# Chunk inverse by Newton steps instead of doubling, one mask and the beta copies dropped, and new planning numbers, in a delta-rule attention and MLP kernel

## Chip, cores, metric

One core of one Trainium2 chip. The metric is device time in microseconds (us), median of several runs, lower is better. "Before" is the kernel that was changed, "after" the changed one. Engines have the names of the profile: PE multiplies matrices (PEld loads its weights), DVE, ACT and POOL work on tiles, and SP issues transfers. An eviction is the copy of a product out of PSUM, the memory that PE writes, by DVE or ACT.

## The reference, cut

```python
batch, n_heads, seq, head_dim = (4, 8, 768, 48)          # 32 heads
k_n = k / (norm(k) + 1e-6)
for t in range(S):                                        # delta rule, one state 48x48 per head
    y[t]  = q[t] @ state
    v_old = k_n[t] @ state
    state = state + beta[t] * outer(k_n[t], v[t] - v_old)
x = y as (3072, 384)
out = gelu_tanh(x @ w_in) @ w_out                         # 384 -> 2048 -> 384
```

## The kernel before

The sequence is cut into 12 chunks of 64 steps. In a chunk, the triangular system that couples its steps, T = (I + N)^-1 with N strictly triangular and 64x64, is solved for each of the 32 heads. The heads go in two groups of 16, so there are 24 chunk-groups. One batch is 16 products of 64x64, one for each head of the group. The inverse of different chunks is independent; the state (R, U, S) goes from chunk to chunk. After every two chunks 512 rows of attention output are ready for the MLP.

The program is not ordered by hand. Each piece of work is given to a planner with a cost for each engine that could do it; the planner places all pieces in time, and the order on each engine is then fixed. The costs matter for nothing else, but a wrong cost gives a bad order.

```python
LAT = {"pe": 0.25, "dve": 0.12, "act": 0.14, "pool": 0.16, "sp": 0.0}
...
late = max(0.0, t - free_at[e])
key = (late > 0.0, t if late > 0.0 else 0.0, o.prio, i)      # ready first, then earliest, then rank
...
def mm_pe(n_ins, cols):
    return {"pe": 0.02 + n_ins * max(0.030, (cols / 2.4 + 32) * 0.5e-3)}
...
# norm of k: the root costs the plan 0.6
op({"pool": 0.6}, {"pool": f_tt(sr[j][:, :], ss[j][:, :], half[:, :], ALU.pow)}, ...)
...
# two masked and scaled versions of K K^T: N (upper) and M (lower)
NU = mU * bcol          # POOL
ML = mL * brow          # POOL; brow is beta broadcast to 64 partitions by DMA, 2 x 256 KB a chunk
M0 = psum * ML          # DVE
N0 = psum * NU          # DVE
DT = psum * mU          # DVE
L1 = I - N0             # POOL
for j in range(0, 6):                # doubling (cut to its data flow)
    [N', L*] = M.T @ [N, L]          # one batch; 128 columns wide for j = 1, 2, 3
    M'       = N.T @ M               # one batch (j <= 4)
    N' evicted by ACT or DVE; L' = L* + L on DVE; M' evicted by ACT or DVE
```

Eleven batches a group, three of them 128 columns wide; DVE does three masks, five additions and a share of the nine plain evictions.

## Time and profile before

| | before |
|---|---|
| median of 4 runs | 403.9 us (402.66 to 407.32) |
| first matmul on K/Q | 52.0 us |
| state update of chunk 1 | 113.2 us |
| state update of chunk 10 | 348.3 us |
| 9 chunks between them | 235.1 us, 26.1 each |
| rest | 55.8 us |

The state updates (DVE, output S) are good milestones, since every chunk has one. I call the time until that of chunk 1 start and ramp, the 9 chunks after it steady state, and the rest the tail.

The page of before, head and slices. A digit is the busy share in a fortieth of the span (10 us); PEclk is the granted TensorE clock in tenths.

```profile
PE 293.8 (73%) x7110; PEld 195.6 (48%) x7110; DVE 256.3 (63%) x389; ACT 146.7 (36%) x247; POOL 163.5 (40%) x112
...
PE   0100062646668969869978979989889999889997
...
DVE  2101267679896965946966857988778797784102
...
POOL 3449358396864741741823533425034110110000
PEclk9999997568588888998979999999999999999999
```

Almost nothing happens on PE for an eighth of the span (1.7 us of work in 52), then it is half busy until slice 12, and from there it is nearly full. DVE is the next busiest in the middle.

The same by stages, from windows of the trace; the columns are window, length, then busy us with instruction counts of PE, PEld, DVE, ACT, POOL, then granted clock, DMA share, GB/s.

```profile
0.00:52.00 52.00, 1.67 (x10) 1.37 (x10) 7.88 (x18) 1.28 (x1) 25.86 (x26) 1.00 0.96 169
52.00:113.20 61.20, 35.73 (x1200) 32.18 (x1200) 48.55 (x69) 21.67 (x38) 45.99 (x29) 0.72 0.76 136
113.20:348.30 235.10, 205.56 (x5196) 132.46 (x5196) 177.56 (x271) 99.12 (x168) 89.28 (x56) 0.94 0.43 81
348.30:404.10 55.80, 50.84 (x708) 29.63 (x708) 22.33 (x34) 24.59 (x42) 2.31 (x2) 1.00 0.12 37
```

In steady state PE is idle for 235.1 - 205.6 = 29.5 us of 235, and DVE is 76% busy. What PE waits for in the whole span (releaser; us, times, longest):

```profile
PE ps L285 <- DMA KQT<-KQ: 41.2, 2, 32.0
PE ps L285 <- DVE NL L269: 22.6, 29, 3.8
```

and in the steady stage alone:

```profile
PE ps L285 <- DVE NL L269: 13.0, 18, 2.5
```

The first is the wait for the transposed K and Q. The second is the addition of L on DVE, one of the steps of the doubling; PE waits there for an eviction. The SP queue around the first transpose (start, us to issue, what):

```profile
39.90 2.11 SPq L293 DMA_DIRECT2D brow<-in_beta_dram  x2
42.06 3.56 SPq L293 DMA_DIRECT2D kf<-in_k_dram  x2
45.66 1.32 SPq L293 DMA_DIRECT2D vf<-in_v_dram  x1
47.02 3.12 SPq L292 DMA_TRANSPOSE KQT<-KQ  x1
```

The transpose of chunk 0 is issued behind the loads of three chunks, with three pairs of beta copies. The groups that the change touches most (busy us, mean ns | PE idle before, releaser):

```profile
L285 PE MATMUL ps<-M,NL 64*64 64x64 bf16 x1920 | 54.9, 202 | 10.2 <-issue 2.9 <-DVE NL L274 2.8 <-ACT M L278 2.3
L285 PE MATMUL ps<-NL,M 64*64 64x128 bf16 x1152 | 48.5, 232 | 17.8 <-DVE NL L269 10.8 <-DVE S L274 4.4 <-DVE M L274 1.0
...
L269 POOL TENSOR_TENSOR ML<-mL,brow 128x1024 f32<-128x1024 f32 x12 | 28.5, 2376 | 18.4 <-DVE M L269 12.5 <-DMA brow<-in_beta_dram 5.8
```

### The profile page before, as it was taken

What the parts mean: (1) busy time and instruction counts of PE and PEld (TensorE: products, weight loads), DVE (VectorE), ACT (ScalarE), POOL (GpSimd) and SP (SyncE); (2) the same over time, 40 slices, a digit from 0 to 9 for tenths busy, and PEclk for the clock granted to TensorE, in tenths of its full rate; (3) what the DMA queues carried; (4) which work ended last, traced back from release to release, by engine and by line L of the source; (5) the groups of instructions that cost most, each with busy time, mean ns of one, the idle gap of its engine ahead of it and who ended that gap; (6) DMA issues with size and microseconds to landing.
All of it is one profiled execution on the core that took longest, in us unless ns stands there. A gap on an engine that the chain in (4) does not pass through costs nothing.

```text
span 404.1 us, 15305 instructions
## 1 busy us (share of the span) xinstructions
PE 293.8 (73%) x7110; PEld 195.6 (48%) x7110; DVE 256.3 (63%) x389; ACT 146.7 (36%) x247; POOL 163.5 (40%) x112
## 2 busy tenths in 40 slices
PE   0100062646668969869978979989889999889997
PEld 0100062645565635645645644656556566565554
DVE  2101267679896965946966857988778797784102
ACT  1000033233355632413734515643067430664260
POOL 3449358396864741741823533425034110110000
PEclk9999997568588888998979999999999999999999
DMA  7998979888279640752722944227122031000302
GB/s 147 181 176 170 172 150 154 162 154 147 52 132 126 124 90 15 159 125 62 143 45 41 185 99 84 33 42 114 60 44 55 3 62 61 4 3 12 108 2 78
DMA packets 141039, 38.14 MB, mean 94 GB/s; under 512 B 135472, under 2 KB 140592, under 8 KB 140976
## 3 DMA queue, kind: packets, MB, share of 16 engines
q1 hardware_dynamic: 138464, 34.02, 44.8%
q0 software_dynamic: 2512, 3.15, 4.8%
q8 instruction: 56, 0.92, 1.0%
q14 instruction: 7, 0.06, 0.0%
HBM read 26.94 MB, written 4.72 MB: 78 GB/s over the span
## 4 chain that ended last, share of the span: by engine, by line
PE 40%; DVE 23%; POOL 20%; DMA 6%; SPq 4%; issue 4%; ACT 1%; DVEq 0%; POOLq 0%
PE ps L285 40%; POOL sr L269 8%; DVE NL L269 6%; POOL ML L269 5%; SPq L293 4%; DMA KQT<-KQ 3%; DVE NL L274 3%; POOL NU L269 3%; DVE M L269 2%; DMA kf<-in_k_dram 2%; POOL sq L269 2%; DVE ss L473 2%; DVE S L269 2%; POOL NL L269 1%; DVE ss L469 1%
## 5 line engine op out<-in xcount | busy, mean ns | idle before, releaser
L285 PE MATMUL ps<-NL,M 64*64 64x128 bf16 (+1 forms) x2304 | 81.5, 219 | 32.0 <-DVE NL L269 22.6
L285 PEld LDWEIGHTS ps<-NL,M 64*64 64x64 bf16 x2304 | 64.9, 118 | 53.3 <-DVE NL L269 31.2
L278 ACT ACTIVATE M<-ps 128x512 bf16<-128x512 f32 x90 | 52.8, 596 | 76.5 <-PE ps L285 76.1
L278 ACT ACTIVATE gT<-ps 128x512 bf16<-128x512 f32 x96 | 57.3, 597 | 62.5 <-PE ps L285 60.2
L285 PE MATMUL ps<-xT,W 128*128 128x512 bf16 x288 | 76.6, 401 | 2.4 <-DVE S L269 1.2
L285 PE MATMUL ps<-W,gT 128*128 128x384 bf16 x384 | 69.8, 331 | 1.7 <-DVE TT L269 0.8
L269 DVE TENSOR_TENSOR NL<-ps,NL 128x512 bf16<-128x512 f32 x96 | 64.4, 684 | 2.9 <-PE ps L285 1.3
L269 POOL TENSOR_TENSOR NL<-idI,NL 128x512 bf16<-128x512 f32 x24 | 27.8, 1160 | 85.9 <-DVE NL L269 85.9
L285 PE MATMUL ps<-M,NL 64*64 64x64 bf16 x1920 | 54.9, 202 | 10.2 <-issue 2.9
L278 ACT ACTIVATE NL<-ps 128x512 bf16<-128x512 f32 x44 | 26.2, 597 | 85.7 <-PE ps L285 85.4
L285 PEld LDWEIGHTS ps<-M,NL 64*64 64x64 bf16 x1920 | 44.6, 117 | 22.6 <-issue 7.3
L285 PEld LDWEIGHTS ps<-W,gT 128*128 128x128 bf16 x384 | 35.2, 99 | 25.4 <-issue 1.0
L285 PE MATMUL ps<-KQT 48*64 48x128 bf16 x384 | 11.7, 239 | 41.4 <-DMA KQT<-KQ 41.2
L269 POOL TENSOR_TENSOR KQ<-kf,rn 128x768 bf16<-128x768 f32 x12 | 17.7, 1474 | 57.0 <-PE ps L285 55.2
L274 DVE CAST NL<-ps 128x512 bf16<-128x512 f32 x52 | 35.2, 687 | 6.9 <-PE ps L285 5.8
L285 PEld LDWEIGHTS ps<-xT,W 128*128 128x128 bf16 x288 | 24.8, 101 | 30.4 <-issue 4.6
L269 POOL TENSOR_TENSOR sr<-ss,half 128x16 f32<-128x16 f32 x12 | 34.9, 2906 | 10.3 <-DVE ss L469 10.3
L269 POOL TENSOR_TENSOR ML<-mL,brow 128x1024 f32<-128x1024 f32 x12 | 28.5, 2376 | 18.4 <-DVE M L269 12.5
L274 DVE COPY osb<-ps 128x384 f32<-128x384 f32 x21 | 11.6, 554 | 32.2 <-PE ps L285 32.1
L285 PEld LDWEIGHTS ps<-KQT 48*64 48x64 bf16 x384 | 7.7, 117 | 45.4 <-DMA KQT<-KQ 41.6
L469 DVE TENSOR_REDUCE ss<-sq 128x16 f32<-128x768 f32 x12 | 11.4, 948 | 28.9 <-POOL sq L269 28.9
L269 DVE TENSOR_TENSOR M<-ps,ML 128x512 bf16<-128x512 f32 x24 | 16.3, 682 | 15.9 <-PE ps L285 15.9
(46 smaller groups left out, 267.9 us busy)
## 6 DMA issues: line engine op xcount, KB each, us to landing
brow<-in_beta_dram SPq DMA_DIRECT2D x24, 256.0 KB, 6.6
kf<-in_k_dram SPq DMA_DIRECT2D x24, 192.0 KB, 4.7
qf<-in_q_dram SPq DMA_DIRECT2D x24, 192.0 KB, 4.3
vf<-in_v_dram SPq DMA_DIRECT2D x24, 192.0 KB, 4.1
out_dram<-osb SPq DMA_DIRECT2D x24, 192.0 KB, 1.9
W<-in_moe_w_in_dram POOLq DMA_DIRECT2D x3, 512.0 KB, 7.9
W<-in_moe_w_out_dram POOLq DMA_DIRECT2D x2, 768.0 KB, 11.5
BL<-in_beta_dram SPq DMA_DIRECT2D x2, 96.0 KB, 3.3
```

The lines of the kernel that those rows point to most:

```text
L269: return lambda e: e.tensor_tensor(out() if callable(out) else out, a() if callable(a) else a, b() if callable(b) else b, op)
L274: return lambda e: e.tensor_copy(out, a() if callable(a) else a)
L278: return lambda e: e.activation(out, a() if callable(a) else a, func)
L285: ins = t.matmul(out, lhsT, rhs, start=st, stop=sp_, skip_group_check=skip)
L293: return lambda e: e.dma_start(out, a)
L469: op({"dve": 0.95}, {"dve": lambda e: e.tensor_reduce(ss[j][:, :], sq[:, :, :], AX.X, ALU.add)}, reads=["sq"], writes=[f"ss{j}"], prio=pr)
L473: op({"dve": 0.1}, {"dve": lambda e: e.tensor_scalar(ss[j][:, :], sr[j][:, :], 1e-6, None, op0=ALU.add)}, reads=[f"sr{j}"], writes=[f"ss{j ...
```

## The change

The inverse becomes five Newton steps, Z' = (2I - Z X) Z with X = (I + N).T, transposed once on PE. Every step has two batches of products, both 64 columns wide, an eviction on DVE (F = 2I - ZX) and one on ACT. Neither M nor the second mask nor the beta copies are needed any more. Beside that: squares and q copies may go to ACT; the root of the first three chunks is a Sqrt on ACT; the output x is evicted by ACT only; intermediate tiles get three buffers. The planner gets new costs, new latencies, a cost for changing between 64x64 and 128x128 matmuls (SWITCH), and a rule that treats work that is late by less than NEAR as ready. The core of the diff, cut:

```diff
-LAT = {"pe": 0.25, "dve": 0.12, "act": 0.14, "pool": 0.16, "sp": 0.0}
+LAT = {"pe": 0.22, "dve": 0.06, "act": 0.06, "pool": 0.08, "sp": 0.0}
+SWITCH = 0.095
+NEAR = {"pe": 0.3, "dve": 0.05, "act": 0.05, "pool": 0.0, "sp": 0.0}
...
-                    key = (late > 0.0, t if late > 0.0 else 0.0, o.prio, i)
+                    far = late > NEAR[e]
+                    key = (far, t if far else 0.0, pr, i)
...
-            op({"pool": 0.6}, {"pool": f_tt(sr[j][:, :], ss[j][:, :], half[:, :], ALU.pow)},
+            if c < NSQ:
+                op({"act": 0.24}, {"act": f_act(sr[j][:, :], ss[j][:, :], ACT.Sqrt)}, ...
+            else:
+                op({"pool": 2.95}, {"pool": f_tt(sr[j][:, :], ss[j][:, :], half[:, :], ALU.pow)}, ...
...
-            op(d_pool2(NP * C), {"pool": f_tt(ML[j][:, :, :], mL..., brow[i][:, :, :], ALU.mult)}, ...
...
-        def mm_pe(n_ins, cols):
-            return {"pe": 0.02 + n_ins * max(0.030, (cols / 2.4 + 32) * 0.5e-3)}
+        def mm_pe(n_ins, cols, tiles=2):
+            t = max(31.0, cols / 2.4 + 3.0) / tiles
+            return {"pe": 1e-3 * n_ins * max(8.3, t)}
...
-            for j in range(0, 6):              # doubling: see above
+            # W = I + N and Z0 = I - N on POOL or DVE; X = W.T by a PE transpose, evicted on ACT
+            for j in range(5):
+                op(mm_pe(16, 64), {"pe": prod(h1, Zo, X)}, ...)
+                op(d_ps(512), {"dve": f_tt(F[:, :, :], bc(twoI), v1(h1), ALU.subtract)}, ...)
+                op(mm_pe(16, 64), {"pe": prod(h2, F, Zo)}, ...)
+                op(d_act(512), {"act": f_act(dst, v1(h2))}, ...)      # dst: Z', at last TT
```

## The prediction

> **What bounds the kernel.** Three stages (busy time by windows of the trace):
> - 0 to 52 us: PE does 1.7 us of work. The first real matmul waits 32 us for the first K/Q transpose (waits). The DMA engines are 0.96 busy with 192- and 256-byte packets; in SP's order the transpose stands behind three chunks of loads and their broadcast-beta copies.
> - 52 to 120 us: PE is busy 40 us of 68, at a granted clock of 0.73; DVE 55, POOL 51. POOL pays per chunk 2.9 (pow), 2.4 (second mask), 1.9, 1.5, 1.5, 0.8 and 2 x 1.16. The first MLP matmul starts at 123.5.
> - 120 to 404 us: PE-bound, 252 us busy of 284; about 26 us a chunk (steps of the S update).
>
> **What changes** (24 chunk-groups; durations from the groups of instructions).
> - PE: before, 11 batches of 16 products a group, three of them 128 columns wide; after, one transpose batch and 10 products, all 64 wide. A 128-wide batch shows 0.63 us, a 64-wide one 0.44: 72 x 0.15 to 0.2 = 11 to 14 us less. MLP (146 us) and state stay.
> - DVE: a group loses one 0.68 mask multiply and its share of evictions (82 x 0.69); x goes to ACT (11.5); some W/Z work comes: 256 to about 190-205 us.
> - ACT: 5.6 evictions a group become 6 (0.6 each); x, some squares and q copies come: 147 to 170-180.
> - POOL: loses the second mask (28.5) and three pows (8.7), shares sq and q copies, makes W and Z0 (2 x 1.16, or on DVE): 163 to 125-140.
> - DMA: 24 x 256 KB of 38 MB go.
> - Longer: the inverse becomes 10 dependent steps of about 0.44 + 0.65 + waits = 1.25 us, plus a transpose prologue: about 16 us a group instead of about 10. Three chunk buffers should hide this, except in the first chunk.
> - Sqrt on ACT costs one or two table loads: about 1283 ns each by the Trainium skill, "ScalarE: Activation LUTs", What ACT_TABLE_LOAD costs; the trace shows 1283. Negligible.
>
> **Critical path.**
> - Start: without 1.5 MB of beta copies for three chunks (9 us at 165 GB/s), and with a shorter norm chain, the first transpose lands at about 38-44 instead of 52: 8 to 14 us.
> - Ramp: POOL no longer limits; first MLP at about 95 instead of 123 in all (another 12 to 18 us net of the longer inverse). The Trainium skill, "TensorE: Matmul & The Clock Gate", Part 1, says that idle time halves the clock; the 0.73 agrees, and a denser ramp should raise it.
> - Steady: PE's 11 to 14 us count nearly in full; planning costs that fit the measured durations (pow planned at 0.6, took 2.9) should save 5 to 10 us of the 32 us of PE idle. Faster DVE and POOL give nothing here by themselves.
> Sum: 10 + 15 + 12 + 8 = 45 to 50 us. Predicted 357 us, range 335 to 379. Chances: faster 0.93, same 0.05, slower 0.02.
>
> **What would show it.** PE busy 275-283 us, above 77% of the span; first K/Q matmul before 45 us; first GELU before 102; DVE near 200; POOL below 140; near 24 us a chunk; no wait on beta loads.
>
> **What would make it wrong.**
> - SP may still place the first transpose behind three chunks: then the start gives under 5 us.
> - The longer chain on in-order ACT, behind GELUs, leaves PE waiting in mid-kernel: 370-385.
> - More switches between 64x64 and 128x128 matmuls (PE idle for "issue") could eat the PE gain.
> - A better plan could bring PE idle after the ramp near nothing: 335.

## The result and the profile after

| | before | after |
|---|---|---|
| median of 4 runs | 403.9 us | 343.4 us (342.62 to 346.65) |
| first matmul on K/Q | 52.0 | 41.3 |
| state update of chunk 1 | 113.2 | 92.8 |
| 9 chunks after it | 235.1 | 198.1 (22.0 each) |
| tail | 55.8 | 50.0 |

All outputs are right. The ratio is 0.851 (95% interval 0.843 to 0.858). Ratios here are the mean time of one kernel's fast runs over that of the other's of the same rounds, so not quite the ratio of the medians that I quote.

The page of after (a slice is 8.5 us):

```profile
PE 266.8 (78%) x7110; PEld 173.4 (51%) x7110; DVE 181.0 (53%) x287; ACT 169.5 (50%) x286; POOL 120.4 (35%) x90
...
PE   0001125875769999898999699999999999999896
...
DVE  2102255786774757676676554666757756642001
...
POOL 5007266443679616057432660160252105000000
PEclk9999999999678999999999699999999999999999
```

By stages, columns as above:

```profile
0.00:41.30 41.30, 1.69 (x10) 1.40 (x14) 6.87 (x21) 8.05 (x11) 13.71 (x19) 1.00 1.11 180
41.30:92.80 51.50, 32.57 (x1363) 29.61 (x1364) 34.72 (x57) 22.57 (x39) 26.99 (x17) 0.93 0.58 95
92.80:290.90 198.10, 187.08 (x5114) 116.83 (x5114) 126.24 (x192) 117.00 (x200) 79.71 (x55) 0.97 0.48 88
290.90:340.90 50.00, 45.49 (x639) 25.58 (x633) 13.21 (x20) 21.84 (x37) 0.00 (x0) 0.99 0.13 41
```

In steady state PE is busy for 187.1 us instead of 205.6, and idle for 11.0 instead of 29.5: busy time and idle time each gave 18.5 us. DVE fell from 76% to 64%.

The clock column needs a caution in the first two stages. In the kept traces the clock's record begins only with its first change, at 59.7 us in before and 67.2 in after, and the view counts time without a record as full clock. The batches of after say otherwise; one of 16 products of 64x64 before and one after that moment:

```profile
66.62 0.62 PE L296 MATMUL ps<-Z,F 64*64 64x64 bf16 x16
69.67 0.42 PE L296 MATMUL ps<-Z,F 64*64 64x64 bf16 x16
```

Batches in a stretch that is recorded at half clock also take 0.61 to 0.64 us (86 to 91 us). If the time before the first record is counted as half clock, my estimate from these records for the ramp is 0.66 in before and 0.68 in after, not 0.72 and 0.93.

The waits of PE, whole span, and then the steady stage alone (DVE F is the step that answers to the addition of L):

```profile
PE ps L296 <- DMA KQT<-KQ: 17.5, 3, 12.2
...
PE ps L296 <- DVE F L280: 1.8, 5, 0.9
```

```profile
PE ps L296 <- DVE F L280: 0.7, 3, 0.3
```

The queue before the first transpose, which still stands behind three chunks of loads, only without the beta copies:

```profile
32.03 2.12 SPq L304 DMA_DIRECT2D qf<-in_q_dram  x2
34.20 1.98 SPq L304 DMA_DIRECT2D vf<-in_v_dram  x2
36.22 3.45 SPq L303 DMA_TRANSPOSE KQT<-KQ  x1
```

And the products; there is no 128-wide group and no second mask any more:

```profile
L296 PE MATMUL ps<-Z,F 64*64 64x64 bf16 x1920 | 54.1, 201 | 7.2 <-issue 5.0 <-DVE F L280 1.8
L296 PE MATMUL ps<-X,Z 64*64 64x64 bf16 x1920 | 52.8, 201 | 8.9 <-ACT Z L289 4.8 <-POOL Z L280 2.4 <-issue 1.3
```

So about 20 us came before chunk 1's state, 37 in steady state and 6 in the tail. The prediction had 25 and 20. The total lies in its range, but steady state gave nearly twice what it said. That is what the experiments are about.

### The profile page after: what moved, and what is told of

Its sections match the earlier page's. It is cut to its first block, busy times and chain, and to the rows that moved or that the text cites. A ratio compares the mean times of both kernels' runs of the same rounds, so it can differ in the third digit from the quotient of the medians.

```text
span 340.9 us, 15121 instructions
## 1 busy us (share of the span) xinstructions
PE 266.8 (78%) x7110; PEld 173.4 (51%) x7110; DVE 181.0 (53%) x287; ACT 169.5 (50%) x286; POOL 120.4 (35%) x90
## 4 chain that ended last, share of the span: by engine, by line
PE 66%; SPq 12%; DMA 8%; ACT 5%; issue 3%; DVE 3%; POOL 1%
PE ps L296 64%; SPq L304 9%; DMA kf<-in_k_dram 7%; SPq L303 2%; ACT Z L289 2%; PE ps L571 2%; ACT x L289 1%; ACT sq L289 1%; DVE F L280 1%; DMA xT<-x 1%; POOL W L280 1%; DVE N L280 1%; DVE R L280 1%; POOL sq L280 0%; POOL Z L280 0%
## 5 line engine op out<-in xcount | busy, mean ns | idle before, releaser
L280 DVE TENSOR_TENSOR F<-twoI,ps 128x512 bf16<-128x512 bf16 x120 | 80.1, 683 | 55.1 <-PE ps L296 54.5
L289 ACT ACTIVATE Z<-ps 128x512 bf16<-128x512 f32 x96 | 55.3, 597 | 39.1 <-PE ps L296 38.7
L296 PE MATMUL ps<-X,Z 64*64 64x64 bf16 x1920 | 52.8, 201 | 8.9 <-ACT Z L289 4.8
L296 PE MATMUL ps<-Z,F 64*64 64x64 bf16 x1920 | 54.1, 201 | 7.2 <-issue 5.0
L280 POOL TENSOR_TENSOR W<-identB,N 128x512 bf16<-128x512 bf16 x21 | 24.2, 1151 | 95.3 <-DVE N L280 95.3
L296 PEld LDWEIGHTS ps<-Z,F 64*64 64x64 bf16 x1920 | 42.6, 115 | 28.7 <-DVE F L280 16.4
L296 PEld LDWEIGHTS ps<-X,Z 64*64 64x64 bf16 x1920 | 42.5, 116 | 25.0 <-ACT Z L289 13.9
L289 ACT ACTIVATE x<-ps 64x768 bf16<-64x768 f32 x24 | 19.3, 804 | 15.7 <-PE ps L296 15.3
L296 PE MATMUL ps<-KQT 48*64 48x128 bf16 x384 | 12.5, 246 | 18.5 <-DMA KQT<-KQ 17.5
L280 POOL TENSOR_TENSOR NU<-mU,bcol 128x1024 f32<-128x1024 f32 x12 | 23.7, 1976 | 1.0 <-DVE bcol L285 1.0
L289 ACT ACTIVATE TT<-ps 128x512 bf16<-128x512 f32 x24 | 14.1, 595 | 18.7 <-PE ps L296 18.6
L280 DVE TENSOR_TENSOR N<-ps,NU 128x512 bf16<-128x512 f32 x24 | 16.3, 686 | 11.8 <-PE ps L296 11.7
```

The lines of the kernel that those rows point to most:

```text
L280: return lambda e: e.tensor_tensor(out() if callable(out) else out, a() if callable(a) else a, b() if callable(b) else b, op)
L289: return lambda e: e.activation(out, a() if callable(a) else a, func)
L296: ins = t.matmul(out, lhsT, rhs, start=st, stop=sp_, skip_group_check=skip)
```

## Experiments

Each was timed in 3 rounds (the last one in 5) beside before on the same chip; before had medians of 403.0 to 404.9 us there, so medians can be compared between the jobs to about half a per cent. My theory after the result was that the gain is about half less work and half a better order. The rivals were that either of them is all of it.

### Control: how far does an accidental order move the time?

```diff
-LAT = {"pe": 0.22,
+LAT = {"pe": 0.23,
```

> A control: one planning latency of the new kernel moved by 0.01 us, no work changed. It shows how far an accidental other order of the same work moves the time. Expected within 1.5%: 338 to 348. If it moves by more than 6 us, differences of that size between other kernels can't be read as causes.

Measured: 347.3 us (343.34 to 348.11). The same work in a slightly different order is 4 us slower in the median. Below, 4 us mean nothing. It is one nudge only: every run below that adds work has another order too, and how far that moves the time is bounded only roughly.

### Work and order apart

The new kernel with all old planning numbers (only one MLP cost, 0.65 for 0.67, stays new):

```diff
-LAT, SWITCH, NEAR, d_ps, d_any, d_act, d_pool2, mm_pe, pow 2.95, reciprocal 0.25   # new
+LAT 0.25/0.12/0.14/0.16, SWITCH 0, NEAR 0, costs of before, pow 0.6, reciprocal 0.2
```

> The new inverse and the new data paths, ordered with all the old planning numbers (old latencies, old costs, no switch cost, no nearness rule). Theory: the 61 us come about half from less work (PE columns, evictions, second mask, beta copies) and half from the order that truer numbers give; then 365 to 382 us, with PE idle after the first 120 us back near 25 us. Rival A, the work alone: 340 to 352. Rival B, the order alone: 392 to 408.

Measured: 362.3 us (ratio 0.896), a little under the range of the theory.

The old kernel with the new planning numbers, rules and matmul kinds; its work is untouched:

```diff
-LAT = {"pe": 0.25, ...}; key = (late > 0.0, ...); pow 0.6; mm_pe old
+LAT = {"pe": 0.22, ...}; SWITCH, NEAR; pow 2.95; mm_pe new
```

> The old kernel with doubling, both masks and the beta copies, ordered with the new planning numbers and rules. Theory: 365 to 382 us, first K/Q matmul still near 50 us, PE idle between 120 us and the last chunk down from 27 us to under 15. Rival A, the work alone: 398 to 408. Rival B, the order alone: 340 to 352.

Measured: 372.9 us (ratio 0.921).

| ratio to before | old numbers | new numbers |
|---|---|---|
| doubling | 1 | 0.921 |
| Newton | 0.896 | 0.851 |

Both rivals fall. The work is worth 10.4% with the old plan and 7.7% with the new (0.851/0.921); the plan is worth 7.9% with the doubling and 5.1% with Newton (0.851/0.896). They overlap: together they save less than the sum. The steady stages of the two runs, first Newton with the old plan, then doubling with the new:

```profile
96.30:303.80 207.50, 188.06 (x5148) 117.58 (x5142) 122.53 (x187) 115.47 (x194) 76.81 (x55) 0.97 0.44 80
```

```profile
100.10:316.80 216.70, 200.49 (x5318) 132.13 (x5312) 174.22 (x269) 111.83 (x192) 109.10 (x68) 0.95 0.54 97
```

The work takes PE busy from 205.6 to 188.1 us; the order takes PE idle from 29.5 to 16.2 us without any change of the work. With the order alone PE's wait for the additions of L on DVE falls from 13.0 to 0.8 us in steady state, although DVE still does them and is busy for 80% of the stage; in the run of doubling with new numbers:

```profile
PE ps L293 <- DVE NL L277: 0.8, 2, 0.7
```

So the long wait for DVE in before came for the most part from the order, and does not show that DVE had too much to do.

### Which part of the plan: costs or rules?

The new kernel with the old costs of instructions, the new latencies and rules:

> The new kernel ordered with the old instruction costs, but the new latencies, switch cost and nearness rule. The old costs hold a batch of 16 products for 0.52 us of PE where the trace shows one every 0.25 us, and the pow for 0.6. Theory: the costs are most of what the plan is worth: 355 to 364, near the 362 of the run with all old numbers. Rival: latencies and rules are: under 348.

Measured: 370.2 us (ratio 0.917), 27 us slower than after and above the range of the theory.

The new kernel with the new costs, and LAT, SWITCH and NEAR as before:

> The new kernel with the new instruction costs but the old latencies, no switch cost and no nearness rule: the fourth corner beside the runs of 343, 362 (all old) and 370 (only costs old). If the costs alone make the order good: 340 to 350. If costs and rules need each other: 355 or more.

Measured: 353.6 us (ratio 0.877), between the two expectations.

The costs matter more, above all with the new rules: 370.2 to 343.4 with the new rules, 362.3 to 353.6 with the old. The rules are worth 10 us with true costs and cost 8 us with wrong ones, so they need the costs. What was wrong with the old costs can be read from the code and the trace. A batch of 16 products of 64 columns cost the old plan 0.02 + 16 x 0.030 = 0.50 us of PE, the new plan 16 x 15.5 ns = 0.25 us. In the trace of after, batches that follow each other start at this distance:

```profile
71.86 0.44 PE L296 MATMUL ps<-X,Z 64*64 64x64 bf16 x16
72.11 0.44 PE L296 MATMUL ps<-Z,F 64*64 64x64 bf16 x16
```

It is 0.25 us; the 0.44 us include the end of the last product, which the next batch covers. The old plan thus charged PE twice the time that these batches take at full clock (at half clock, before 67 us, they follow each other at 0.43 us). That it therefore saw PE as full and had no reason to bring another group's batch forward is my reading of the planner, and no run shows it. In the steady stage of the run with old costs PE is busy 196 and idle 23 us of 219:

```profile
94.70:314.00 219.30, 196.32 (x5152) 120.96 (x5152) 118.53 (x180) 113.39 (x193) 81.46 (x58) 0.96 0.41 76
```

I did not separate PE's costs from those of the other engines.

### What of the work: narrower products?

Three products of each group are 128 columns wide again; the second half is unread:

```diff
-    {"pe": prod(h2, F, Zo)},  alloc=[(h2, 1)]
+    wide = j in (1, 2, 3)     # rhs = both Z buffers, 128 columns; ACT evicts the half that counts
+    {"pe": f_mms(pw) if wide else prod(h2, F, Zo)},  alloc=[(h2, 2 if wide else 1)]
```

> The new kernel with three of the ten products of each group made 128 columns wide again (the other half of the result unread; the output stays right). Theory: PE is the limit in steady state, so the 72 wide batches cost 10 to 15 us: 353 to 359. Rival: the narrower products were hidden in PE idle time and give nothing: under 347. A wide product also takes two PSUM banks; if banks are what limits, over 362.

Measured: 348.8 us. PE busy rose by 8.8 us (275.6 instead of 266.8), the time by 5.4 us over after and by 1.5 over the control. Between the two expectations, and near the limit of what the control lets one read. The prediction counted 11 to 14 us "nearly in full". The products themselves did rise by about that: the group Z,F takes 66.3 us instead of 54.1. The rest of PE took less, at a higher mean granted clock (0.990 instead of 0.969), so the 8.8 us understate the work.

### What of the work: the load of DVE?

The change took 75 us of work from DVE. Here four extra multiplies a group go back to it, each bound between two F steps:

```diff
+                if j < 4:
+                    op(d_ps(512), {"dve": f_tt(scr, NU[j2][:, ps_, :], mU..., ALU.mult)},
+                       reads=[nm["F"], f"NU{j2}"] + MASKU, writes=["scr"], prio=pj + 0.15)
```

> The new kernel with four extra DVE multiplies a group (128x512, about 0.6 to 0.7 us each, into a tile that nobody reads), placed between the F steps: gives DVE back the roughly 60 us that the change took from it. The prediction said that a faster DVE gives nothing in steady state by itself: then under 349. Rival, suspected since the wide products cost only some 5 us: DVE, in order, was where the products of before waited, and its relief is a main part of the gain: 355 or more, with PE idle for DVE F up from 2 us to over 10.

Measured: 372.9 us (ratio 0.925), 29.5 us slower than after. The multiplies took 79 us in all, 0.82 each, more than I expected. Chunk 1's state came at 106.1 instead of 92.8 us, steady state took 207.2 instead of 198.1, the tail 56.7 instead of 50.0. So 13.3 us were lost before chunk 1's state, 9.1 in steady state and 6.7 in the tail. PE's wait for DVE F rose from 1.8 to 8.5 us over the span, less than the 10 of the expectation. The steady stage:

```profile
106.10:313.30 207.20, 193.62 (x5207) 121.92 (x5205) 170.61 (x244) 120.37 (x207) 93.38 (x61) 0.93 0.43 81
```

The same multiplies, free of the F steps and of low rank:

```diff
-                       reads=[nm["F"], f"NU{j2}"] + MASKU, writes=["scr"], prio=pj + 0.15)
+                       reads=[f"NU{j2}"] + MASKU, writes=["scr"], prio=pj + 6.0)
```

> The same 96 extra DVE multiplies as in the run that came to 373 us, but bound to no F step and of low rank: no product waits for them, other than by DVE being busy. If DVE's load is what costs (in-order DVE, each extra multiply delaying a ready eviction by up to 0.8 us): 358 or more. If the longer chain cost it (four times 0.8 us more between the products of a group): under 350.

Measured: 357.0 us (ratio 0.884), 13.6 us slower than after, a hair under the first expectation. Its steady stage:

```profile
89.20:304.90 215.70, 193.90 (x5281) 123.14 (x5278) 185.12 (x269) 127.90 (x217) 96.63 (x58) 0.94 0.44 84
```

PE is idle 21.8 us there instead of 11.0, DVE is 86% busy, and PE's wait for DVE F is 6.4 us in this stage, where after has 0.7. This looks like the cost of DVE's load alone, but the run does not show that. The free multiplies read the mask NU, so POOL could not overwrite a mask buffer before they were done, and it waited 24 us for them in 3 places. The longest wait came before the mask of chunk 3 (start, us, what, idle before and releaser):

```profile
79.95 1.93 POOL L280 TENSOR_TENSOR NU<-mU,bcol 128x1024 f32<-128x1024 f32 x1 [20.10 <-DVE scr L280]
```

In after this mask is made at 63.4 us. Chunk 3's state then comes at 150.7 us instead of 131.4, and that is more than the whole loss. From chunk 3's state to chunk 10's nothing more is lost; first after, then this run:

```profile
131.40:290.90 159.50, 152.68 (x4229) 95.51 (x4224) 100.83 (x153) 92.67 (x160) 54.64 (x39) 0.98 0.42 79
150.70:304.90 154.20, 142.34 (x3889) 89.69 (x3884) 130.84 (x192) 93.01 (x159) 62.09 (x38) 0.96 0.42 78
```

DVE is 85% busy there instead of 63%, with 53 of the 96 multiplies. PE is idle for 11.9 us instead of 6.8 and waits 5.2 us for DVE F instead of 0.5. So in these seven chunks the load costs about 5 us of PE idle, about what the control moved the time; the two stretches do not hold quite the same PE work. The bound multiplies took 165.0 us for the same chunks, and the control 157.3. What the load costs in the start and ramp, and how the 29.5 us divide between load and longer path, stays open.

The run with the bound multiplies shows one thing more. Its PE work is exactly that of after, yet PE is busy 283.4 us instead of 266.8, at a mean granted clock of 0.902 instead of 0.969. The records show when the clock falls: in before, after and this run PE was at most 73% busy in the 3.4 us before each change to half clock, and at least 88% busy before each change back (not counting the change at the very end). This run has 71.7 us recorded at half clock, after 20.5. So here a PE that waited more also worked slower, and part of the fall in "PE busy" from 293.8 (clock 0.924) to 266.8 is no removed work.

### What of the work: beta copies and the second mask?

```diff
+                load_brow(c + 2, T(c - 1, 1))                    # 2 x 256 KB a chunk again
+            op(d_pool2(NP * C), {"pool": f_tt(brow[j], mU..., brow[j], ALU.mult)}, ...)
-               reads=[h, f"NU{j2}"], writes=[nm["N"]]
+               reads=[h, f"NU{j2}", brow0, brow1], writes=[nm["N"]]     # N waits for it, value unread
-        NOSB = 4
+        NOSB = 3                                                  # room for two beta buffers
```

> The new kernel with the 24 beta copies (256 KB each) loaded again and the second mask multiplied on POOL again; the first product of a group waits for it, its value is unread, the output stays right. To fit the memory: two beta buffers instead of three, the multiply in place, three output tiles instead of four. Theory, as in the prediction: beta copies and mask cost the start about 9 us and the ramp a few more, in steady state nothing: 354 to 362, first K/Q matmul at 48 to 53 instead of 41. Rival: both were off the path: under 348.

Measured: 370.5 us (ratio 0.919), 27 us slower than after; I had expected 11 to 19. Its first two stages:

```profile
0.00:47.70 47.70, 1.65 (x6) 1.35 (x6) 6.70 (x21) 7.42 (x10) 14.59 (x20) 1.00 1.08 177
47.70:111.70 64.00, 34.58 (x1326) 31.37 (x1328) 34.61 (x53) 24.83 (x41) 39.42 (x24) 0.84 0.73 130
```

The first K/Q matmul comes at 47.7 instead of 41.3 us, chunk 1's state at 111.7 instead of 92.8, so 19 us are lost before steady state, nearly all that the change gained there (20.4). Steady state took 204.7 us (6.6 more; the control 2.8 more), where nothing was expected, and the tail 52.7. I did not separate the copies from the mask, and two beta buffers instead of three make the later copies come later.

### What of the work: the root on ACT

```diff
-        RL, RB, NSQ = 3, 3, 3
+        RL, RB, NSQ = 3, 3, 0
```

> The new kernel with the pow on POOL for all chunks, no square root on ACT. The pow takes 2.9 us instead of 0.2. Theory: in the start POOL waits for loads anyway, so at most 4 us are lost: 341 to 348. Rival: POOL's chain sets the start: 350 or more, first K/Q matmul 3 us or more later.

Measured: 342.0 us, the same as after. The first K/Q matmul came 3.2 us later (44.5), and chunk 1's state at the same time (93.2). The Sqrt is worth nothing at the end.

### A version that beats both

After still begins real work at 41 us, and the waits show that PE stands for transposes. First another order of the start, with the same work:

```diff
-        load_step(0, -70)                      # k, q, v of chunk 0, then BL, then chunk 1
+        load_step(0, -70, "kq")                # v loads later, after the first q cast
-        weight loads at the start of POOL's queue
+        weight loads after KQ1 and KQ2 are made
+        loads of chunk 2 after the first q cast; the copy of v on POOL after KQ2
```

> The new kernel with another order of the start, the same work: the weight loads (3 MB) are issued only after the third chunk's K is normalized, the v loads of the first two chunks after the first q cast, the copy of v on POOL after that, and the loads of the third chunk no longer ahead of the first transpose. Theory: the first K/Q matmul waits for bytes that it does not need; it should come at 20 to 28 us instead of 41, and half or more of that should reach the end: 325 to 336. Rival: what the start gains is lost again waiting for weights or for the following chunks: 339 or more.

Measured: 342.2 us. The first K/Q matmul came at 31.0 us (20 to 28 expected), and still nothing was gained: the rival held. The trace shows where it went (start, us, what, idle before and releaser, PE only):

```profile
36.43 0.64 PE L567 MATMUL ps<-identB,W 64*64 64x64 bf16 x16
44.30 1.07 PE L296 MATMUL ps<-KQT 48*64 48x128 bf16 x32 [7.23 <-DMA KQT<-KQ]
45.15 0.63 PE L296 MATMUL ps<-Z,F 64*64 64x64 bf16 x16
```

At 36.4 us chunk 0's inverse is under way. Then PE, in its fixed order, stands 7.2 us before products of chunk 1, whose transpose is late, and the next step of chunk 0 comes behind them. Why the plan put them there is again my reading: it costs a 192 KB load at 0.6 us and a transpose at 1.1 us of queue; the trace of after shows loads at 1.0 us apiece (2.0 for two) and that transpose at 3.45. So the costs of transfers were mended too:

```diff
-                    op({"sp": 0.6}, {"sp": f_dma(t[s]...            # load of 192 KB
+                    op({"sp": 1.2}, ...
-            op({"sp": 1.1}, {"sp": f_dma(KQT[i]...  prio=pr + 0.2, lat=4.0)
+            op({"sp": 3.2}, ...                     prio=pr - 1.0, lat=2.5)
+        xT transpose 2.2 instead of 1.1; loads of chunk c+2 follow the q cast of chunk c-1;
+        W1 after KQ2, W2 after chunk 3's K
```

> The other order of the start again, now planned with transfer costs that the trace shows: 1.2 us of queue for a 192 KB load instead of 0.6, 3.2 for a K/Q transpose instead of 1.1; the transposes go ahead of loads of the same time, the loads of later chunks follow the q cast that frees their place, and the weights come in two steps. In the run of 342 us with the first order PE, in order, stood before products of the second and third chunk whose transposes were late, while the first chunk's inverse could have run. Theory: with truer transfer costs the plan puts the first chunk's products first, and the 10 us won at the start reach the end: 328 to 338, the first state update before 66 us instead of 76. Rival: the ramp is limited by the bytes of the loads in any order: 339 to 347.

Measured: 325.8 us (321.46 to 329.58, 6 runs; ratio 0.800, 95% interval 0.795 to 0.805), below the expected range. Three of the six runs, the profiled one too, count as slow because they are over 1.5% above the fastest; the ratio uses the three fast ones alone. The first two stages of the profiled run:

```profile
0.00:15.50 15.50, 1.65 (x6) 1.36 (x6) 5.74 (x18) 5.45 (x7) 6.29 (x11) 1.00 0.88 150
15.50:74.30 58.80, 38.67 (x1298) 34.79 (x1300) 35.90 (x56) 26.12 (x43) 32.06 (x25) 1.00 1.15 175
```

Chunk 1's state comes at 74.3 instead of 92.8 us; steady state (196.8) and tail (52.6) are much as in after. The 1.00 of the second stage is no measured clock: this trace has no record before 72.6 us. Several things were changed at once here against the run before, order and costs, so the costs are not shown to be the only cause; what is shown is that the start has no lower limit at 41 us.

## Why the prediction was right

- **The total.** 357 predicted, 343.4 measured, inside 335 to 379. Direction and chance of "faster" were right. That it lies inside is partly luck: one term was too large and two were too small, as follows.
- **Start, 10 us.** Right: 52.0 to 41.3. The named causes act there: with beta copies and second mask back it comes at 47.7 (6.4 of the 10.7 us), with the pow back at 44.5 (3.2). The gain belongs to the work and not to the planning numbers: 41.4 with Newton and all old numbers, 54.9 with doubling and the new. But the prediction also said that the start would give under 5 us if the transpose stayed behind three chunks. It stayed there, and the start gave 10.7. The loads of a fourth chunk (4.9 us of queue), which stood before it in before and no longer do, were not in the sum. The "shorter norm chain" gave nothing at the end (342.0 without it).
- **Ramp, 15 us.** Over-sized: from the first K/Q matmul to chunk 1's state the time went from 61.2 to 51.5 us, 9.7 us. The first MLP matmul came at 102.3 us, not at about 95, and the first GELU at 104.3, not before 102.
- **PE's narrower products, 11 to 14 us "nearly in full".** The work was sized about right (12.2 us in the group when put back), the effect was not: it cost 1.5 to 5.4 us of time.
- **Steady state, 12 + 8 us.** Under-sized, work and plan alike. In this stage the work saved 27.6 us with the old plan and 18.6 with the new (12 predicted), the plan 18.4 with the doubling and 9.4 with Newton (5 to 10 predicted). Over the whole span the order alone gave 31 and 19 us. The prediction found one wrong cost (the pow) and did not compare the most frequent one, the batch of products, with the trace: 0.50 us in the plan, 0.25 in the trace. What in the work gave more than the narrower products is shown only in part.
- **"Faster DVE and POOL give nothing here by themselves."** Not settled. Bound between the products, extra DVE work of about the size that was removed costs 29 us, of which 9.1 in steady state; but it lengthens the path too. Free of the F steps it costs 14 us, which are lost by chunk 3's state, where POOL stood 20.1 us for it. The Trainium skill, "TensorEngine Tiling (Array Packing)", section PSUM Bottleneck, says that once tiling has sped up the matmuls, the copy out of PSUM may become the bottleneck. The waits look like that at first (before waited 13.0 us for DVE's additions in steady state, after 0.7), but the other order of the same work left 0.8, so this does not bear it out. For POOL, mask and beta copies together cost 6.6 us in steady state, and were not separated.
- **Counts.** PE busy 266.8 (predicted 275 to 283), DVE 181 (about 200), POOL 120 (below 140), 78% of the span (above 77), 22.0 us a chunk (24). What fell short in the ramp was outweighed by steady state, so the sum came out better than its parts.
- **Clock.** As the prediction quotes from the Trainium skill, "TensorE: Matmul & The Clock Gate", Part 1, idle time lowers the clock. The traces agree: their records hold only half and full clock, and the changes follow PE's busy share as told above (at most 73% before a fall, at least 88% before a rise). That the denser ramp would raise the clock is not shown: with the unrecorded time as half clock, the estimate is 0.66 before and 0.68 after.

The separate costs (27, 29, 5, and 19 for the plan) add to more than the 60 us of the whole. They overlap, each comes with an order of its own, and no exact division of the gain is claimed.

## What to carry to other kernels

When a planner fixes the order, check its costs against the trace first, transfers and the most frequent batch above all: here a third to a half of the gain, and 18 us beyond it, lay in numbers and order and not in the work. A wait for an engine does not show that the engine has too much to do: another order of the same work took the wait for DVE's additions from 13.0 to 0.8 us. When work is put back as a test, look where in the span the time is lost, and what else had to wait for the added work. Earlier data help only if no in-order engine then stands before something else that is still late.

## What the Trainium skill lacked or had wrong

- "TensorE: Matmul & The Clock Gate", Part 1, says that the start-to-start of matmuls never drops below about 25 ns, and does not exempt small matmuls that are packed into parts of the array, which the page treats in a part of its own. For these it does drop lower: 16 products of 64x64 on two tiles follow in 0.25 us (15.6 ns each, shown above), and 32 products of 48 columns on four tiles in 0.27 us (8.4 ns each), from these lines of after:

```profile
75.83 0.44 PE L296 MATMUL ps<-U,KQ 64*64 64x48 bf16 x32
76.10 0.22 PE L296 MATMUL ps<-U,DT 64*64 64x48 bf16 x4
```

- The same Part 1 gives no share of busy time at which the clock is halved. In before, after and the run with bound DVE work PE was 0 to 73% busy in the 3.4 us before a fall (over 20% in 16 of 17), so it need not stand still.
- No page that I found speaks of the stretches of up to 2.7 us in which PE waits for nothing that the profile shows ("issue", 10.5 us in 11 places in after). No run here settles their cause.
